# Moving x and g by 64 or 128 bytes in SBUF, with the weights left where they are

## The chip, the cores and the metric

The kernel runs on one core of a Trainium2 chip. The metric is the time of one execution in microseconds (us) on the device. Three runs of the kernel before gave 848.03, 845.73 and 847.87 us, a median of 847.87 us. TensorE (PE) does the matrix products, with its loads of the stationary operand shown apart as PEld; VectorE (DVE), ScalarE (ACT) and GpSimd (POOL) do the elementwise work; SyncE (SP) issues most transfers. SBUF is the on-chip memory that all of them read. An address in it here means the byte offset within a partition, which is the same in all 128 partitions.

## The reference

```
attn_out[b,h] = (scale * q k^T * D[h]) v          D[h][i,j] = gamma[h]**(i-j) for i >= j, else 0
x   = attn_out laid out as 2304 tokens x 512
h   = x @ w_in                                    2304 x 2048
g   = h * tanh(softplus(h))
y   = g @ w_out                                   2304 x 512
logits = y @ w_gate                               2304 x 8
every token goes to one of 8 experts, greedily by logit, at most 288 tokens to an expert
out[tokens of e] = relu(y[tokens of e] @ w1[e]) @ w2[e]
```

All of it is float32.

## The kernel before, in words

The program has two parts, one after the other. The first (`first_part`) computes the attention, the dense layer and the logits. The second (`second_part`) sorts the tokens to experts and runs the experts. No tile of the second part changes its address with this change.

Every float32 operand of the large products is split into a high part and a rest (names ending in h and l), both stored as fp32r, and a product is three products: high by high, low by high, high by low. One matmul is a load of a 128x128 stationary operand (LDWEIGHTS) and a stream of the moving operand through it (MATMUL).

The tokens are cut into 9 blocks of 256 (n = 0 to 8) and the hidden layer into 16 slices of 128 (f = 0 to 15). A pair (n, f) is a step; there are 144. `plan()` mixes the steps of blocks 0 to 2, since their weights are still arriving and being split; from block 3 on the blocks follow each other. A step issues:

- `ff_h` (line 317): 12 matmuls, 4 slices of the 512 inputs by 3 products. Stationary is a 128x128 piece of `winh[f]` or `winl[f]`, moving are 256 columns (1024 bytes) of `xh` or `xl`. They run in the order winh·xh, winl·xh, winh·xl.
- `ff_a1` to `ff_b3`: the activation g and its split into `gh` and `gl`, on ACT (lines 326 to 328 and 358), DVE (334, 339, 352) and POOL (346, 347, 359).
- `ff_y` (line 411), three steps later: 6 matmuls. Here a half of `gh` or `gl` is stationary and 512 columns (2048 bytes) of `woh[f]` or `wol[f]` move. In the last block `ff_y_last` (line 447) does it the other way round: 12 matmuls with pieces of the weights stationary and 256 columns of `gh` or `gl` moving.

The attention of a later block is put between the steps of an earlier one (lines 219 to 281). The order on each engine is the order in which the code is written.

The second part's expert products are line 1257 (stationary `wxh`/`wxl`, moving 288 columns, 1152 bytes, of `xth`/`xtl`) and line 1271 (the same with `hth`/`htl`).

The addresses come from pools that hand out tiles one behind the other. In the program before, all 64 weight tiles of the first part (`winh`, `winl`, `woh`, `wol`) begin at 160 modulo 256, and `xh`, `xl`, `gh`, `gl`, the temporaries `d` and `u`, `pm`, `y`, `att` and the raw weights at 96. A slice of x is 1024 bytes and a slice of a weight 512, so every piece read has the same remainder as its tile. In the second part a slice of `xth` or `hth` is 1152 bytes, four and a half times 256, so the slices begin in turn at 96 and at 224, and all stationary pieces begin at 96.

`x_block` gives each block its x: block 2 has its own two tiles in the pool `stage`, all others take turns on two buffers of the pool `work`.

Of the kernel before, what the change touches and what calls it, by code (L numbers as in the profile page):

```python
# [7 lines left out]
F32 = mybir.dt.float32  # L8
F32R = mybir.dt.float32r
# [9 lines left out]
P = 128  # L19
# [4 lines left out]
TB = 256  # L24
NB = N // TB
KT = DM // P
# [55 lines left out]
def first_part(ctx, tc, att, att_ht, att_hn, dtab, qtab, ktab, stab, wi, wo, wgb, ydram, L, constants, cst, begin, grid):  # L82
    nc = tc.nc
    big = ctx.enter_context(tc.tile_pool(name="big", bufs=1))
    work = ctx.enter_context(tc.tile_pool(name="work", bufs=1))
# [41 lines left out]
    for n, f in sorted([(i, f) for i, (n, f) in enumerate(steps) if n == 0 for f in (f, f + NF)],  # L127
                       key=lambda p: (p[0] + (WOL if p[1] >= NF else 0), p[1])):
        parts.append((wo[f - NF], woh[f - NF], wol[f - NF]) if f >= NF
                     else (wi[f], flat(winh[f]), flat(winl[f])))  # L130
    raws = []
    y0 = work.tile([P, 2, DM], F32, tag="y", name="y0")
    cvs = [y0[:, 0, :], y0[:, 1, :]]
    done = [0]
# [42 lines left out]
            nc.gpsimd.tensor_sub(self.lo, self.t, self.hi.bitcast(F32))  # L177

    xT = {}

    def x_block(n):
        if n not in xT:
            if n == 2:
                xT[n] = [sp.tile([P, KT, TB], F32R, tag="x2", name=f"x{k}2", bufs=2) for k in "hl"]
            else:
                xT[n] = [work.tile([P, KT, TB], F32R, tag="x" + k, name="x" + k, bufs=2) for k in "hl"]
        return xT[n]

    pm = {}
# [45 lines left out]
    def a_out(ci):  # L235
        b, s0, n = CHUNKS[ci]
        a = at_tiles[ci]
        qT = a[:, 0, 0:4 * n].rearrange("p (h t) -> p h t", h=4)
        p = pm[ci]
        xp = bank()  # L240
        for hp in range(4):
            if s0 > 0:
                nc.tensor.matmul(xp[:, hp, :n], SD[:, hp, :], qT[:, hp, :], start=(hp == 0), stop=False,
                                 skip_group_check=True)
        for hp in range(4):
            for s in range(2):
                h = 2 * hp + s
                nc.tensor.matmul(xp[s * 64:(s + 1) * 64, hp, :n], a[:n, 3, h * D:(h + 1) * D],  # L248
                                 p[:n, s, hp, :n], start=(s0 == 0 and hp == 0), stop=True,
                                 skip_group_check=True)  # L250
        tok = b * S + s0
        xh, xl = x_block(tok // TB)
        o = tok % TB
        nc.scalar.activation(xh[:, :, o:o + n], xp[:, :, :n], AF.Copy)
        nc.vector.tensor_sub(xl[:, :, o:o + n], xp[:, :, :n], xh[:, :, o:o + n].bitcast(F32))  # L255
# [53 lines left out]
    def ff_h(n, f, i):  # L309
        xh, xl = x_block(n)  # L310
        if i % 2 == 0:
            hbank[0] = psum.tile([P, 2, TB], F32, tag=("ph0", "ph1")[i // 2 % 2], name="ph")
        ph = hbank[0][:, i % 2, :]
        k = 0
        for kt in range(KT):
            for w, x in ((winh, xh), (winl, xh), (winh, xl)):
                nc.tensor.matmul(ph, w[f][:, kt, :], x[:, kt, :], start=(k == 0), stop=(k == 11))  # L317
                k += 1
        q2[n, f] = ph
# [211 lines left out]
    for i in range(len(steps) + YL):  # L531
# [13 lines left out]
        if new:  # L545
            n, f = steps[i]
# [873 lines left out]
def build(tc, ap, out):  # L1420
    nc = tc.nc
    with ExitStack() as ctx:
        pp = ctx.enter_context(tc.tile_pool(name="pp", bufs=1))
        dp = ctx.enter_context(tc.tile_pool(name="dp", bufs=1, space=bass.MemoryType.DRAM))
        cp = ctx.enter_context(tc.tile_pool(name="cp", bufs=1))
        ctx.enter_context(tc.manual_schedule())
        L = pp.tile([P, NT, E], F32, name="L")
        ydram = dp.tile([N, DM], F32, name="ydram")
        cst = {}
        start = []  # L1430
        cs = ExitStack()

        def begin():
            start.append(Search(cs, tc, L, cst))
            return start[0].early()

        with ExitStack() as c1:
            first_part(c1, tc, ap["att"], ap["att_ht"], ap["att_hn"], ap["dtab"], ap["qtab"],
                       ap["ktab"], ap["stab"], ap["wi"], ap["wo"], ap["wgb"], ydram, L, lambda: constants(cp, tc, ap, cst), cst, begin, lambda *a: Grid(cs, tc, L, cst).pieces(*a))
        keep = ctx.enter_context(tc.tile_pool(name="keep", bufs=1, reuse_waits="tile"))  # L1440
        L0 = keep.tile([P, NT, E], F32, name="L0")
        nc.gpsimd.tensor_copy(L0, L)
        with ExitStack() as c2:
            flag = second_part(c2, tc, L, ydram, ap["wx"], cst, out, start[0], True, L0)
            again = nc.values_load(flag[0:1, 0:1], min_val=0, max_val=1)
        cs.close()
        with tc.If(again != 0):
            with ExitStack() as c3:
                general_constants(c3, tc, ap, cst)
                second_part(c3, tc, L0, ydram, ap["wx"], cst, out, Start(c3, tc, L0, cst), False)  # L1450
# [91 lines left out]
```

## Time and profile before

| | us |
|---|---|
| median of three runs | 847.87 |
| the profiled execution | 849.51 |
| its span, first to last instruction | 847.6 |
| TensorE busy in the span | 776.6 |
| weight loads busy | 709.3 |
| DVE, ACT, POOL busy | 548.1, 437.3, 475.1 |

The profile shows one execution. Busy times overlap between engines. [...] A step of 12 matmuls on line 317 takes about 1.4 us from start to start of the next thing.

### The profile page before, as it was taken

The page shows a single profiled execution, that of the slowest core. Times are in us where ns is not written, and L with a number is a line of the kernel's source. Part 1 is how long each engine was busy: PE and PEld are TensorE (multiplying, and loading weights), DVE is VectorE, ACT ScalarE, POOL GpSimd, SP SyncE. Part 2 cuts the span into 40 slices and gives each one's busy share as a digit, 9 for nine tenths or more (in the row PEclk, how much of TensorE's full clock was granted, in tenths as well). Part 3 has the DMA queues.
Part 4 walks back from the last instruction along what each step waited for, and adds up shares of the span by engine and source line. Part 5 has one row for each costly group of instructions (what it writes and reads, how often), then busy time and mean ns, then how long its engine had stood idle before and what let it go on. Part 6 is the DMA issues. An engine that isn't in the chain of part 4 may idle for free.

```text
span 847.6 us, 16248 instructions
## 1 busy us (share of the span) xinstructions
PE 776.6 (92%) x6151; PEld 709.3 (84%) x6151; DVE 548.1 (65%) x1271; ACT 437.3 (52%) x963; POOL 475.1 (56%) x541
## 2 busy tenths in 40 slices
PE   6688878899999999999999999939999999999993
PEld 5677667788998888888888889929989899999993
DVE  4797989865545699797897885576566654442110
ACT  2677878754554545455455554423444543554520
POOL 2533333365544567676666665414777986977811
PEclk9799999999999999999999999958999999999997
DMA  8536343101204210120110000044555655655411
GB/s 313 174 111 201 137 135 125 50 27 51 75 26 150 76 50 26 61 82 34 51 50 26 1 26 2 2 147 163 171 181 178 194 168 174 177 159 175 128 30 32
DMA packets 27320, 87.63 MB, mean 103 GB/s; under 512 B 4448, under 2 KB 5600, under 8 KB 27104
## 3 DMA queue, kind: packets, MB, share of 16 engines
q1 hardware_dynamic: 24160, 77.06, 27.9%
q0 software_dynamic: 3072, 9.44, 3.5%
q8 instruction: 50, 0.82, 0.4%
q14 instruction: 38, 0.31, 0.1%
HBM read 77.05 MB, written 9.44 MB: 102 GB/s over the span
## 4 chain that ended last, share of the span: by engine, by line
PE 72%; DVE 9%; issue 6%; DMA 5%; ACT 4%; POOL 2%; SPq 0%; DVEq 0%; POOLq 0%; ACTq 0%
PE ph L317 20%; PE hp L1257 10%; PE op L1271 8%; PE b_E L411 8%; PE b_F L411 7%; DMA raw<-in_wi_dram 2%; PE cnt L972 2%; PE b_A L219 1%; DVE r L339 1%; PE b_D L248 1%; DVE raw L163 1%; DVE hot L868 1%; POOL wxl L811 1%; DMA raw<-in_wo_dram 1%; PE b_E L447 1%
## 5 line engine op out<-in xcount | busy, mean ns | idle before, releaser
L317 PE MATMUL ph<-xh,winh 128*128 128x256 f32 x576 | 164.9, 286 | 9.4 <-ACT d L326 6.7
L317 PE MATMUL ph<-xl,winh 128*128 128x256 f32 x576 | 162.9, 283 | 0.2 <-DVE xl L255 0.2
L317 PE MATMUL ph<-xh,winl 128*128 128x256 f32 x576 | 163.0, 283 | 0.0
L811 POOL TENSOR_TENSOR wxl<-wraw,wxh 128x1024 fp32r<-128x1024 f32 x60 | 142.4, 2396 | 30.5 <-ACT wxh L809 30.0
L359 POOL TENSOR_TENSOR gl<-u,gh 128x256 fp32r<-128x256 f32 x114 | 85.8, 753 | 88.3 <-ACT gh L358 87.6
L317 PEld LDWEIGHTS ph<-xh,winh 128*128 128x128 f32 x576 | 110.4, 192 | 20.2 <-ACT d L326 7.0
L326 ACT ACTIVATE d<-ph 128x256 f32<-128x256 f32 x144 | 54.8, 381 | 133.0 <-PE ph L317 117.3
L317 PEld LDWEIGHTS ph<-xh,winl 128*128 128x128 f32 x576 | 110.8, 192 | 4.5
L317 PEld LDWEIGHTS ph<-xl,winh 128*128 128x128 f32 x576 | 111.1, 193 | 0.4 <-DVE xl L255 0.4
L339 DVE RECIPROCAL u<-u 128x128 f32<-128x128 f32 x113 | 107.7, 953 | 3.9
L334 DVE TENSOR_TENSOR u<-d 128x128 f32<-128x128 f32 x113 | 45.4, 402 | 63.3 <-ACT d L328 55.5
L346 POOL TENSOR_TENSOR u<-d,u 128x128 f32<-128x128 f32 x112 | 52.3, 467 | 52.9 <-DVE u L339 52.8
L809 ACT ACTIVATE wxh<-wraw 128x1024 fp32r<-128x1024 f32 x64 | 67.3, 1052 | 18.5 <-DMA wraw<-in_wx_dram 18.5
L327 ACT ACTIVATE d<-d,half_b 128x256 f32<-128x256 f32 x144 | 73.5, 510 | 4.7
L347 POOL TENSOR_TENSOR u<-d,u 128x128 f32<-128x128 f32 x112 | 68.2, 609 | 8.8
L328 ACT ACTIVATE d<-d 128x256 f32<-128x256 f32 x144 | 60.2, 418 | 4.6
L358 ACT ACTIVATE gh<-u 128x256 fp32r<-128x256 f32 x144 | 57.9, 402 | 2.1 <-DVE u L352 2.0
L368 DVE SCALAR_TENSOR_TENSOR scr<-y,WG 128x512 bf16<-128x512 f32 x64 | 55.2, 863 | 0.4
L1248 DVE SCALAR_TENSOR_TENSOR htl<-hp,hth 128x288 fp32r<-128x288 f32 x64 | 28.4, 454 | 40.2 <-ACT hth L1260 37.9
L1260 ACT ACTIVATE hth<-hp 128x288 fp32r<-128x288 f32 x64 | 26.1, 408 | 51.9 <-PE hp L1257 46.7
L352 DVE SCALAR_TENSOR_TENSOR u<-u,ph 128x256 f32<-128x256 f32 x144 | 52.5, 365 | 0.3
L177 POOL TENSOR_TENSOR wol<-y,woh 128x512 fp32r<-128x512 f32 x16 | 20.6, 1288 | 53.5 <-ACT woh L174 53.5
(271 smaller groups left out, 1931.0 us busy)
## 6 DMA issues: line engine op xcount, KB each, us to landing
wraw<-in_wx_dram SPq DMA_DIRECT2D x64, 512.0 KB, 4.4
att<-in_att_dram SPq DMA_DIRECT2D x32, 512.0 KB, 5.4
raw<-in_wi_dram SPq DMA_DIRECT2D x16, 512.0 KB, 3.9
raw<-in_wo_dram SPq DMA_DIRECT2D x16, 512.0 KB, 3.2
ydram<-y SPq DMA_DIRECT2D x9, 512.0 KB, 2.8
WG<-in_wgb_dram SPq DMA_DIRECT2D x1, 2048.0 KB
att<-in_att_ht_dram SPq DMA_DIRECT2D x4, 256.0 KB, 4.4
att<-in_att_hn_dram SPq DMA_DIRECT2D x4, 256.0 KB, 4.8
```

The source lines that it names most:

```text
L317: nc.tensor.matmul(ph, w[f][:, kt, :], x[:, kt, :], start=(k == 0), stop=(k == 11))
L327: nc.scalar.activation(df, df, AF.Square, bias=half_b, scale=-0.5)
L328: nc.scalar.activation(df, df, AF.Copy, bias=0.5, scale=0.5)
L339: nc.vector.reciprocal(r, r)
L347: eng.tensor_mul(u[:, 0, :], d[:, 1, :], r)
L358: nc.scalar.activation(gh, g, AF.Copy)
L359: eng.tensor_sub(gl, g, gh.bitcast(F32))
L411: nc.tensor.matmul(py[n][t], g[:, t * P:(t + 1) * P], w[f], start=(f == 0 and w is woh and g is gh), stop=(f == NF - 1 and g is gl))
L809: nc.scalar.activation(hi, raw, AF.Copy)
L811: rest = lambda eng: eng.tensor_sub(lo, raw, hi.bitcast(F32))
L1257: nc.tensor.matmul(hp, W[kt][w][:, s], x[:, kt, :], start=(k == 0), stop=(k == 11))
L1271: nc.tensor.matmul(op, W[4 + ft // 2][w][:, s], h[:, ft, :], start=(k == 0), stop=(k == 23))
```

## The change

A tile of 64 bytes that nothing uses is put into the pool `work` ahead of `y0`. The two buffers of x are no longer handed out by the pool block by block; they are four tiles made once, and the second tile of the first pair has 128 bytes of padding behind it. What is written into them, who reads them and when is the same.

```
+    work.tile([P, 16], F32, name="between")
     y0 = work.tile([P, 2, DM], F32, tag="y", name="y0")
...
+    xs = [[work.tile([P, KT * TB + o], F32R, name=f"x{k}{j}")[:, :KT * TB].rearrange("p (k t) -> p k t", k=KT)
+           for k, o in (("h", 0), ("l", e))] for j, e in enumerate((32, 0))]
...
-                xT[n] = [work.tile([P, KT, TB], F32R, tag="x" + k, name="x" + k, bufs=2) for k in "hl"]
+                xT[n] = xs[n if n < 2 else (n + 1) % 2]
```

The addresses that follow, modulo 256, as the built programs have them:

| tiles | before | after |
|---|---|---|
| weights `winh`, `winl`, `woh`, `wol` | 160 | 160 |
| x of blocks 0, 3, 5, 7 | 96 | 160 |
| x of blocks 1, 4, 6, 8 | 96 | 32 |
| x of block 2, raw weights | 96 | 32 |
| `gh`, `gl`, `d`, `u`, `pm` | 96 | 32 |
| `y`, `y0` | 96 | 160 |
| `att`, all of the second part | 96 and others | the same |

So the moving operand of line 317 begins 64 bytes behind its stationary one modulo 256 before; after, it begins at the same remainder (blocks 0, 3, 5, 7) or 128 bytes away (the other blocks). For lines 411 and 447 the distance goes from 64 to 128 bytes.

Engine by engine the two programs hold the same instructions in the same order with the same shapes; x's tiles have other names. One wait differs: in the second part POOL waits for a mark of PE ahead of the product that writes `wxl7` and no longer ahead of the one before it, which writes `wxl6` (line 811).

## Rows read from the trace of the kernel before

**Rows 1.** The page: span, and busy time of TensorE.
```profile
span 847.6 us, 16248 instructions
...
PE 776.6 (92%) x6151; PEld 709.3 (84%) x6151; DVE 548.1 (65%) x1271; ACT 437.3 (52%) x963; POOL 475.1 (56%) x541
```
**Rows 2.** The page's chain of waits, shares by engine.
```profile
PE 72%; DVE 9%; issue 6%; DMA 5%; ACT 4%; POOL 2%; SPq 0%; DVEq 0%; POOLq 0%; ACTq 0%
```
**Rows 3.** Stretches of the span: busy us of each engine, clock, DMA.
```profile
core 0: us, PE busy (x) PEld busy (x) DVE busy (x) ACT busy (x) POOL busy (x), PEclk, DMA share, GB/s
0.00:200.00 200.00, 164.16 (x1175) 140.60 (x1176) 153.05 (x280) 133.71 (x306) 76.48 (x83) 0.95 0.39 135
200.00:500.00 300.00, 300.00 (x2289) 268.25 (x2288) 229.92 (x458) 154.16 (x382) 185.94 (x284) 1.00 0.16 54
500.00:545.00 45.00, 43.15 (x358) 42.01 (x357) 26.25 (x62) 23.85 (x59) 23.63 (x42) 1.00 0.04 13
```
**Rows 4.** What TensorE waited for from 200 to 545 us: total, times, longest.
```profile
PE b_D L638 <- DVE g_mm L634: 1.0, 1, 1.0
PE b_E L447 <- POOL gl L359: 0.5, 2, 0.3
PE b_E L447 <- ACT gh L358: 0.4, 1, 0.4
```
**Rows 5.** Groups on TensorE, 200 to 545 us: count, busy us, mean ns.
```profile
L317 PE MATMUL ph<-xh,winh 128*128 128x256 f32 x404 | 113.2, 280 | 0.0
L317 PE MATMUL ph<-xh,winl 128*128 128x256 f32 x404 | 112.8, 279 | 0.0
L317 PE MATMUL ph<-xl,winh 128*128 128x256 f32 x404 | 112.7, 279 | 0.0
```
**Rows 6.** Line 317 from 492.7 to 493.4 us: ns min/median/max, starts.
```profile
L317 PE MATMUL ph<-xl,winh x3: 277/277/277, 492.4 to 493.1; 128*128 128x256 f32 x3
L317 PE MATMUL ph<-xh,winh x3: 276/276/277, 492.6 to 493.2; 128*128 128x256 f32 x3
```
**Rows 7.** Line 317 from 515 to 540 us, the same columns.
```profile
L317 PE MATMUL ph<-xh,winh x36: 280/281/282, 516.1 to 539.7; 128*128 128x256 f32 x36
...
L317 PE MATMUL ph<-xh,winl x36: 281/282/282, 516.2 to 539.9; 128*128 128x256 f32 x36
```
**Rows 8.** Timeline of TensorE around 493 us: start us, us.
```profile
492.32 0.28 PE L317 MATMUL ph<-xh,winl 128*128 128x256 f32 x1
...
493.57 0.39 PE L411 MATMUL b_E<-woh,gh 128*128 128x512 f32 x1
...
494.95 0.28 PE L317 MATMUL ph<-xh,winh 128*128 128x256 f32 x1
```
**Rows 9.** Timeline of TensorE around 517 us.
```profile
516.07 0.28 PE L317 MATMUL ph<-xh,winh 128*128 128x256 f32 x1
...
517.49 0.28 PE L447 MATMUL b_E<-gh,woh 128*128 128x256 f32 x1
```
**Rows 10.** Line 411 from 200 to 500 us: ns min/median/max, starts.
```profile
L411 PE MATMUL b_F<-wol,gh x86: 387/394/398, 199.8 to 499.8; 128*128 128x512 f32 x86
L411 PE MATMUL b_E<-woh,gl x85: 388/392/452, 200.0 to 497.2; 128*128 128x512 f32 x85
```
**Rows 11.** Line 447 from 500 to 545 us, the same columns.
```profile
L447 PE MATMUL b_E<-gh,wol x29: 276/281/283, 502.4 to 544.3; 128*128 128x256 f32 x29
```
**Rows 12.** Timeline of TensorE in the second part, around 820 us.
```profile
815.11 0.68 PE L1257 MATMUL hp<-xtl,wxh 128*128 128x288 f32 x4
...
819.27 1.20 PE L1271 MATMUL op<-hth,wxh 128*128 128x288 f32 x8
...
823.43 0.30 PE L1271 MATMUL op<-hth,wxl 128*128 128x288 f32 x1
```
**Rows 13.** Line 1271 from 819.6 to 823.3 us: ns min/median/max.
```profile
L1271 PE MATMUL op<-hth,wxl x8: 291/292/293, 820.3 to 821.2; 128*128 128x288 f32 x8
```
**Rows 14.** Line 811 from 540 to 600 us: ns min/median/max.
```profile
L811 POOL TENSOR_TENSOR wxl<-wraw,wxh x4: 2384/2394/2402, 582.2 to 590.8; 128x1024 fp32r<-128x1024 f32 x4
```

## The prediction

> **What bounds the kernel now.** I read the stretches of the span first. [...] Before 200 us TensorE is busy for 164 of 200 us [rows 3], and the chain there runs through transfers, DVE and ACT as well as matmuls, so I count nothing for it. The second part begins when the first has ended, and none of its tiles moves, so what the first part gains or loses should arrive at the end in full. Over the span the chain is 72% TensorE [rows 2], which is busy 776.6 us [rows 1].
>
> Then I read how long matmuls of one shape take, since the change can only act there. Line 317 has 3 x 404 = 1212 matmuls from 200 to 545 us, of 279.3 ns on average [rows 5]. They come in two levels. Around 493 us they take 276 or 277 ns [rows 6], and 11 of them start within 493.57 - 492.32 = 1.25 us [rows 8], one per 113.6 ns. From 516 us on they take 280 to 282 ns [rows 7], and 12 start within 517.49 - 516.07 = 1.42 us [rows 9], one per 118.3 ns. The addresses are the same at both levels, modulo 256, so the level isn't set by the address alone. Going by the durations, (279.3 - 276.5) / (281.5 - 276.5) = 0.56 of the 1212 are at the slow level, and the mean distance is 113.6 + 0.56 x 4.7 = 116.2 ns.
>
> **What the change touches.** No instruction is added, removed or moved. The change can act in four ways.
>
> *Line 317.* The moving x begins 64 bytes from its stationary weights modulo 256 before, and 0 (blocks 3, 5, 7) or 128 bytes away after (blocks 4, 6, 8). No row of the first part shows such a distance, but the second part does: its moving slices begin at 96 and 224 in turn, and all its stationary pieces at 96. There 64 matmuls of 288 columns start from 815.11 to 823.43 us [rows 12], one per 130.0 ns, half at distance 0 and half at 128, and the durations lie within 291 to 293 ns [rows 13], so the two distances cannot be far apart. To bring 130.0 ns to 256 columns I take the cost of a column from lines 411 and 317 of one stretch: six matmuls of 512 columns start within 494.95 - 493.57 = 1.38 us, 230.0 ns each [rows 8]; (230.0 - 113.6) / 256 = 0.455 ns a column, 14.6 ns for 32 columns. At the slow level it is (230.0 - 118.3) / 256 = 0.436 ns, 14.0 ns. So line 317 would take 115.4 to 116.0 ns a matmul after; I take 115.7, against 116.2 now: 1212 x -0.5 = -0.6 us. The bounds are the two levels seen at this shape: all fast, 1212 x (113.6 - 116.2) = -3.2 us; all slow, 1212 x (118.3 - 116.2) = +2.5 us. It is nearest to the middle because the two halves of the blocks get the two distances in equal number.
>
> *Lines 411 and 447.* Line 411 has about 6 x 85.5 = 513 matmuls from 200 to 500 us, with a median near 394 ns, a least of 387 and a most of 398 in a typical group [rows 10]. Its distance goes from 64 to 128. Bounds: 513 x -7 ns = -3.6 us, 513 x +4 ns = +2.1 us. No row shows this shape at another distance, and the spread lies on both sides, so I take 0. Line 447 (172 matmuls, median 281, least 276, most 283 [rows 11]) can gain 172 x 5 ns = 0.9 us or lose 172 x 2 ns = 0.3 us; I take 0.
>
> *DVE, ACT, POOL and the transfers.* Their tiles move by 64 or 128 bytes too. From 200 to 545 us TensorE waits 1.9 us for them, and a gain or loss there hides behind it. Elsewhere DVE, ACT and POOL hold 9 + 4 + 2 = 15% of the chain [rows 2], 127 us. No row shows one operation at two such addresses; the nearest is the spread of equal POOL products, 2384 to 2402 ns, 0.8% [rows 14], which bounds it at ±1.0 us. I take 0, as the shapes and the number of bytes stay.
>
> *The wait that POOL shifts.* It is for a mark of PE from the first part and stands before products that start at 582 us or later [rows 14], long after line 317 has ended. It costs nothing in either place; behind it on POOL stand only the later products of line 811 and the expert gathers.
>
> **The sum.** -0.6 us. The profiled execution took 849.51 us, 847.6 of span and 1.9 around it, and would become 848.9. It lies 1.6 us above the median of the runs, 847.87; off that median the forecast is 847.3 us. The outer bounds added are -3.2 - 3.6 - 0.9 - 1.0 = -8.7 us and +2.5 + 2.1 + 0.3 + 1.0 = +5.9 us.
>
> The trace shows that a load of weights runs beside nearly every matmul, PEld 268 of 300 us [rows 3], and that equal matmuls at equal addresses differ by 4.7 ns. [...]
>
> [...]
>
> **The rivals.**
>
> *Faster: the fast level holds.* If the slow level comes from the moving stream meeting the weight load at a fixed distance of 64 bytes, the new distances could avoid it. Then line 317 and line 447 run at the fast level (-3.2 and -0.9 us), and line 411 gains up to its best (-3.6 us): 847.9 - 4.1 = 843.8 us, or 840.2 us with all of line 411. For it: the levels hold for long stretches without a change in the work, from 516 to 540 us for one [rows 7], as a fixed pattern of two reads would. Against it: the second part runs at 0 and 128 and is not at a rate that would be the fast level (130.0 - 14.6 = 115.4 against 113.6). It decides from 0.8 of the 1212 at the fast level on with some gain on line 411; line 317 alone at the fast level is just 3.2 us.
>
> *Slower: distance 128 pins the slow level.* Half the blocks' line 317, and all of lines 411 and 447, get distance 128. If that is the bad one, these products run at the slow level or above: 606 x +2.1 = +1.3 us on blocks 4, 6 and 8, +2.1 us on line 411, +0.3 us on line 447, and should distance 0 be bad as well another +1.3 us: 851.6 to 852.9 us. For it: the second part's 115.4 to 116.0 ns is a mean over both distances, and one half could hide a worse one. Against it: durations there spread by 2 ns only [rows 13]. It decides once line 411 joins; line 317 alone stays within the noise.
>
> *The address changes what others do.* If the reads of TensorE meet those of DVE, ACT and POOL, all of which moved along, the levels would fall elsewhere but in the same mixture: within 1 us of 847.9, the forecast's side.
>
> **How the numbers follow.** What a measurement of this kernel can tell from no change is about 0.3%, 2.5 us; the runs shown span 2.3 us. No change that can be told, with the rule of the ports and the last rival in it: 0.44, at 847.3 us, its own range 845.3 to 850.3 us. Faster, 0.33: the levels are seen, and 840 to 845 us is within reach of them. Slower, 0.23: its bounds are nearer. The range of 842.0 to 851.5 us leaves out a deeper gain (about 0.1) and the slower rival at its worst (about 0.08).
>
> **What would show it.** Right: line 317 from 200 to 545 us at a mean of 278.5 to 279.5 ns, blocks at distance 0 and at 128 within 3 ns of each other, line 411 near 394 ns, and TensorE still without a gap. Wrong towards faster: a mean of 277 ns or less, or a median of line 411 at 390 ns or below. Wrong towards slower: 281 ns or more, line 411 at 397 ns or more. If matmuls stay as they are and the time moves by over 2.5 us, the cause is not on TensorE in that stretch and the whole reading is wrong.

## The result: 851.2 us, and the profile after

The kernel after took 851.2 us in the median (849.37 to 853.57, eight runs), against 847.87 us before (eight runs); the ratio of the means is 1.0051, with a 95% interval of 1.0037 to 1.0065. The kernel after is slower by 3.3 us between the medians and by 4.3 us, 0.5%, between the means, where no change was forecast.

TensorE has no gap after either. The stretches of the kernel after, with the columns of [rows 3]:

```profile
200.00:500.00 300.00, 300.00 (x2266) 268.64 (x2265) 227.40 (x454) 152.28 (x376) 184.02 (x280) 1.00 0.16 54
500.00:545.00 45.00, 43.63 (x360) 42.80 (x358) 25.73 (x60) 24.05 (x60) 23.66 (x43) 1.00 0.04 13
```

It is as busy as before and does less: 2266 matmuls from 200 to 500 us, where it was 2289 [rows 3]. The clock is the same 1.00, so the matmuls themselves follow each other more slowly. Their durations on line 320, which was line 317, from 200 to 545 us (ns min/median/max, first and last start):

```profile
L320 PE MATMUL ph<-xh,winh x402: 276/283/285, 199.8 to 542.4; 128*128 128x256 f32 x134
L320 PE MATMUL ph<-xh,winl x402: 279/283/287, 199.9 to 542.5; 128*128 128x256 f32 x134
L320 PE MATMUL ph<-xl,winh x402: 274/283/290, 200.0 to 542.6; 128*128 128x256 f32 x134
```

The median of all three is 283 ns, above the most that the slow level showed before [rows 7]. The starts say by how much: matmuls of 283 ns that start some 120 ns apart overlap, so the pace is the time from start to start. Four starts in the kernel after: a step of block 6 (x at distance 128) from its first matmul to what follows it, and one of block 7 (distance 0):

```profile
430.20 0.28 PE L320 MATMUL ph<-xh,winh 128*128 128x256 f32 x1
...
431.64 0.40 PE L414 MATMUL b_E<-woh,gh 128*128 128x512 f32 x1
...
451.25 0.28 PE L320 MATMUL ph<-xh,winh 128*128 128x256 f32 x1
...
452.68 0.49 PE L246 MATMUL b_D<-att,sd 128*128 128x128 f32 x3
```

12 matmuls in 1.44 us and in 1.43 us: 120.0 and 119.2 ns each, against 113.6 and 118.3 at the two levels of before [rows 8, 9]. Line 414, which was 411, hardly moves; from 200 to 500 us it has, beside [rows 10],

```profile
L414 PE MATMUL b_F<-wol,gh x84: 390/392/393, 208.1 to 499.2; 128*128 128x512 f32 x84
L414 PE MATMUL b_E<-woh,gl x84: 390/396/398, 208.3 to 499.4; 128*128 128x512 f32 x84
```

with medians of 392 and 396 where they were 394 and 392.

One number serves to compare all kernels below: the time from the first matmul of block 3 to the first matmul of the last step, 95 steps later. TensorE runs through it with next to no wait: from 200 to 545 us it waited 1.9 us before [rows 4] and 1.4 us after. The timeline of the kernel before at these two places:

```profile
220.55 0.28 PE L317 MATMUL ph<-xh,winh 128*128 128x256 f32 x1
...
538.68 0.28 PE L317 MATMUL ph<-xh,winh 128*128 128x256 f32 x1
```

and of the kernel after:

```profile
219.37 0.28 PE L320 MATMUL ph<-xh,winh 128*128 128x256 f32 x1
...
541.33 0.28 PE L320 MATMUL ph<-xh,winh 128*128 128x256 f32 x1
```

318.1 us became 322.0 us, +3.8 us. From the starts in the trace, line 317's matmuls in blocks 3 to 8 go from a mean of 116.2 to 119.2 ns, line 411's from 230.6 to 231.3 (where nothing stands between them) and line 447's from 116.6 to 118.9. In the stretch that is 1140 x 3.0 = 3.4 us, 498 x 0.7 = 0.3 us and 144 x 2.3 = 0.3 us: some 4 us for 3.8. The two profiled spans differ by 1.7 us only, since block 3 began 1.2 us earlier after, and from the last step to the end of the span it took 0.9 us less; in the medians of the runs 3.3 us stand.

The starts also show a rhythm for each distance between the addresses. In blocks 3, 5 and 7, at distance 0, 87% of the matmuls follow the one before by 119 to 121 ns. In blocks 4, 6 and 8, at 128, the times from start to start go 117, 120, 123, 117, 120, 123, or 115, 117, 122, 120, 119. Both have a mean of 119.2 ns. Before, they were mostly 113 to 114 or 117 to 118 for many matmuls on end.

### The profile page after: what moved, and what is told of

The parts are those of the page before. It is cut to its first block, busy times and chain, and to the rows that moved or that the text cites. A ratio compares the mean times of both kernels' runs of the same rounds, so it can differ in the third digit from the quotient of the medians.

```text
span 849.3 us, 16248 instructions
## 1 busy us (share of the span) xinstructions
PE 782.8 (92%) x6151; PEld 714.6 (84%) x6151; DVE 547.6 (64%) x1271; ACT 438.0 (52%) x963; POOL 475.4 (56%) x541
## 4 chain that ended last, share of the span: by engine, by line
PE 71%; DVE 10%; issue 6%; DMA 5%; ACT 4%; POOL 2%; SPq 0%; DVEq 0%; POOLq 0%; ACTq 0%
PE ph L320 20%; PE hp L1260 9%; PE op L1274 8%; PE b_E L414 8%; PE b_F L414 7%; DMA raw<-in_wi_dram 2%; PE cnt L975 2%; DVE r L342 2%; PE b_A L222 1%; PE b_D L251 1%; DVE raw L164 1%; DVE hot L871 1%; DMA raw<-in_wo_dram 1%; PE b_E L450 1%; PE b_F L450 1%
## 5 line engine op out<-in xcount | busy, mean ns | idle before, releaser
L329 ACT ACTIVATE d<-ph 128x256 f32<-128x256 f32 x144 | 55.0, 382 | 137.2 <-PE ph L320 117.0
L1260 PE MATMUL hp<-xth,wxh 128*128 128x288 f32 x256 | 50.1, 308 | 0.9 <-DVE htl L1251 0.9
```

The source lines that it names most:

```text
L1260: nc.tensor.matmul(hp, W[kt][w][:, s], x[:, kt, :], start=(k == 0), stop=(k == 11))
```

## The experiments

Theory: the time of a 256-column matmul goes by the distance, modulo 256, between the address of the moving operand and that of the stationary pieces being loaded. Rivals: x's own address modulo 256; the form of x's tiles, made once; the moved tiles of the other engines. All edits are made to the kernel before, if nothing else is said. Each ratio is one of means, against the kernel before run beside it, whose medians were 848.95 us (e1 to e4), 846.89 (e5 to e8), 848.36 (e9 to e12) and 848.85 us (e13, e14). "Stretch" is the time just defined, and each run's two starts stand behind it. A remainder written as a distance is moving minus stationary on line 317; "behind" is negative.

**e1_static: the new tiles without the new addresses.**

```
-    work.tile([P, 16], F32, name="between")          (from the kernel after)
-    ... enumerate((32, 0))]
+    ... enumerate((0, 0))]
```

> The kernel after with both paddings taken out: x in four tiles made once, every address as before (x and g at 96). If the addresses do it: line 317 (here L319) at 116.2 ns a matmul from 200 to 545 us as before, and 847.9 us, ratio 1.000. If the form of x's tiles did it: 119.2 ns a matmul as in the kernel after, and 851 us, ratio 1.005.

849.05 us against 848.95, ratio 1.0002 (0.9990 to 1.0015); line 317 at 116.2 ns. Stretch 318.2 us:

```profile
220.61 0.28 PE L319 MATMUL ph<-xh,winh 128*128 128x256 f32 x1
...
538.80 0.28 PE L319 MATMUL ph<-xh,winh 128*128 128x256 f32 x1
```

The form of the tiles costs nothing.

**e2_dist0 and e3_dist128: one distance for all blocks.**

```
+    work.tile([P, 16], F32, name="between")          e3: 48
     y0 = work.tile([P, 2, DM], F32, tag="y", name="y0")
```

> The kernel before with 64 bytes of padding ahead of y0 alone: x and g at 160, distance 0 to the weights in all blocks and in lines 411 and 447. If the distance modulo 256 between moving and stationary sets it: line 317 in every block as blocks 3, 5 and 7 of the kernel after, an even 120 ns with a mean of 119.2, so 1212 x 3.0 ns = +3.6 us, ratio about 1.004. If only distance 128 is bad: 116 ns or less and 848 us or below. If it is the moving of the other engines' tiles: between 848 and 851 us with line 317 at 116 ns.

> The kernel before with 192 bytes of padding ahead of y0 alone: x and g at 32, distance 128 everywhere. If the distance sets it: line 317 in every block as blocks 4, 6 and 8 of the kernel after, 117, 120 and 123 ns in turn with a mean of 119.3, +3.7 us, ratio about 1.004. If only distance 0 is bad: 116 ns and 848 us.

Distance 0: 853.69 us, ratio 1.0062 (1.0047 to 1.0077), line 317 at 119.3 ns. The second and third line below are the first matmuls of two steps of its last block, one step apart (12 matmuls of line 317 and 12 of line 447); the first and last line bound its stretch of 322.1 us:

```profile
219.99 0.28 PE L318 MATMUL ph<-xh,winh 128*128 128x256 f32 x1
...
519.01 0.28 PE L318 MATMUL ph<-xh,winh 128*128 128x256 f32 x1
...
521.89 0.28 PE L318 MATMUL ph<-xh,winh 128*128 128x256 f32 x1
...
542.05 0.28 PE L318 MATMUL ph<-xh,winh 128*128 128x256 f32 x1
```

24 matmuls in 2.88 us are 120.0 ns each, in a place where the kernel before ran at 118.3 [rows 9]. Distance 128: 854.5 us, ratio 1.0067 (1.0052 to 1.0081), 119.3 ns, stretch 322.4 us:

```profile
221.81 0.28 PE L318 MATMUL ph<-xh,winh 128*128 128x256 f32 x1
...
544.23 0.28 PE L318 MATMUL ph<-xh,winh 128*128 128x256 f32 x1
```

Both distances are bad, and equally so.

**e4_shift_all: new addresses, old distance.**

```
+    big.tile([P, 16], F32, name="ahead")
     winh = [big.tile([P, KT, P], F32R, name=f"winh{i}") for i in range(NF)]
```

> The kernel before with 64 bytes of padding ahead of the first weight: weights at 224, x, g and all behind at 160, so that x lies where it lies in blocks 3, 5 and 7 of the kernel after, but at the old distance of 64 to the weights. If the distance sets it: 116.2 ns a matmul and 847.9 us, ratio 1.000. If x's own address modulo 256 sets it (160 is bad, 96 good): 119.2 ns and 851.5 us, ratio 1.004.

849.1 us, ratio 1.0005 (0.9993 to 1.0018), line 317 at 116.3 ns, stretch 318.3 us:

```profile
220.22 0.28 PE L318 MATMUL ph<-xh,winh 128*128 128x256 f32 x1
...
538.54 0.28 PE L318 MATMUL ph<-xh,winh 128*128 128x256 f32 x1
```

With x at 160, where the kernel after has it in half its blocks, nothing is lost so long as the weights stand 64 bytes further on. The distance counts, not x's own address.

**e5 to e9: the other distances.** The edit is that of e2_dist0 with 32, 8, 24 and 40 in place of 16; for 96 behind, `half_b` is made ahead of `winh` and nothing else is changed.

> The kernel before with 128 bytes of padding ahead of y0: x and g at 224, that is 64 bytes ahead of the weights modulo 256, where they were 64 behind. If what counts repeats every 128 bytes (0 and 128 alike, as measured at 119.2 and 119.3 ns): line 317 as before, 113.5 and 118 ns in turn with a mean of 116, ratio 1.000. If 64 behind is one good place in 256: 119 ns or more, ratio 1.004 or more.

> The kernel before with 32 bytes of padding ahead of y0: x and g at 128, 32 behind the weights modulo 256. If the cost falls evenly from distance 0 to distance 64: between 116.2 and 119.2 ns a matmul, 117.7, ratio 1.002. If the cost comes in steps of 64 bytes: 116.2 or 119.2 ns, ratio 1.000 or 1.004.

> The kernel before with 96 bytes of padding ahead of y0: x and g at 192, 32 ahead of the weights. If the sign of the distance plays no part: as with 32 behind. If it does, this differs from 32 behind by more than 1 ns a matmul on line 317.

> The kernel before with the 4-byte tile half_b made ahead of the weights instead of behind them: weights at 192, x and g at 96 still, 96 behind modulo 256. If the cost repeats every 128 bytes, 96 behind is 32 ahead: the same mean on line 317 as in the run at 32 ahead, within 0.5 ns. If it repeats every 256 only, no such match.

> The kernel before with 160 bytes of padding ahead of y0: x and g at 0, 96 ahead of the weights modulo 256, the last of the eight distances in steps of 32. If every distance has its own mean, as the seven measured so far: between 116.1 and 119.4 ns a matmul on line 317, ratio 1.000 to 1.007, and 64 behind stays the best. If 96 ahead lies between its neighbours 64 ahead (117.8) and 128 (119.3): 118.5 ns, ratio 1.005.

The starts, in the order e5, e6, e7, e8, e9, and then all eight distances (g moves with x; lines 411 and 447 as above):

```profile
220.44 0.28 PE L318 MATMUL ph<-xh,winh 128*128 128x256 f32 x1
...
541.39 0.28 PE L318 MATMUL ph<-xh,winh 128*128 128x256 f32 x1
```
```profile
221.53 0.28 PE L318 MATMUL ph<-xh,winh 128*128 128x256 f32 x1
...
542.45 0.28 PE L318 MATMUL ph<-xh,winh 128*128 128x256 f32 x1
```
```profile
221.01 0.28 PE L318 MATMUL ph<-xh,winh 128*128 128x256 f32 x1
...
540.63 0.28 PE L318 MATMUL ph<-xh,winh 128*128 128x256 f32 x1
```
```profile
220.98 0.28 PE L318 MATMUL ph<-xh,winh 128*128 128x256 f32 x1
...
542.75 0.28 PE L318 MATMUL ph<-xh,winh 128*128 128x256 f32 x1
```
```profile
221.37 0.28 PE L318 MATMUL ph<-xh,winh 128*128 128x256 f32 x1
...
544.73 0.28 PE L318 MATMUL ph<-xh,winh 128*128 128x256 f32 x1
```

| distance | kernel | line 317, ns | line 411 | line 447 | stretch, us | ratio (95%) |
|---|---|---|---|---|---|---|
| -96 | e8 | 118.5 | 233.2 | 118.4 | 321.8 | 1.0062 (1.0043 to 1.0081) |
| -64 | before | 116.2 | 230.6 | 116.6 | 318.1 | 1 |
| -32 | e6 | 118.4 | 231.6 | 118.0 | 320.9 | 1.0053 (1.0039 to 1.0068) |
| 0 | e2 | 119.3 | 231.4 | 119.6 | 322.1 | 1.0062 (1.0047 to 1.0077) |
| 32 | e7 | 117.0 | 232.8 | 116.8 | 319.6 | 1.0023 (1.0010 to 1.0036) |
| 64 | e5 | 117.8 | 233.5 | 117.8 | 321.0 | 1.0057 (1.0043 to 1.0071) |
| 96 | e9 | 120.2 | 232.9 | 119.8 | 323.4 | 1.0075 (1.0059 to 1.0091) |
| 128 | e3 | 119.3 | 231.8 | 118.6 | 322.4 | 1.0067 (1.0052 to 1.0081) |

64 behind, where the kernel before stands, is the best of the eight, and the only one with a stretch at 113 to 114 ns; 64 ahead has 117 to 118 throughout. So what counts repeats neither every 64 nor every 128 bytes: 96 behind and 32 ahead differ by 1.5 ns. The expectation that the cost falls evenly from 0 to 64 behind was wrong: 32 behind, at 118.4, is close to distance 0. Of the other forecasts, that 32 ahead and 32 behind differ by more than 1 ns came true (e7); e5 fits neither of its two, and e9, at 120.2, lies above the most that was expected of it. The ratios are up to 0.2% above what the stretches give (e3: 4.3 of 848 us is 0.5%, measured 0.67%). For e5 to e8 some of that lies in the kernel before, which ran 1.5 to 2.1 us faster beside them than beside the others. For the rest no cause is shown: in e3's trace block 3 begins 1.3 us later than before (221.81 against 220.55 us), but in the trace of the kernel after, whose line 317 is as slow in blocks 0 to 2 (119.0 ns), 1.2 us earlier.

**e10_g_only: the other tiles alone.** Behind x's tiles 192 bytes are left free, so that g, d and u lie as in the kernel after, with x in place (but for block 2).

```
     a_out(0)
+    work.tile([P, 48], F32, name="between")
```

> The kernel before with 192 bytes of padding behind x: x of all blocks but 2 stays at 96, g, d and u move to 32 as in the kernel after. If line 317's reads of x carry the loss: 116.2 ns a matmul on line 317, 231.2 on line 411, 119 on the last block's line 447 (192 x 2.3 ns = 0.4 us), ratio 1.000 to 1.001. If the moving of g, d and u carries it: ratio 1.003 or more.

849.39 us, ratio 1.0008 (0.9998 to 1.0018), stretch 318.7 us:

```profile
220.75 0.28 PE L317 MATMUL ph<-xh,winh 128*128 128x256 f32 x1
...
539.49 0.28 PE L317 MATMUL ph<-xh,winh 128*128 128x256 f32 x1
```

Line 447 went to 118.9 ns, as in the kernel after, line 411 stayed at 230.3. Line 317 took 119.3 ns in block 2, whose x had moved to distance 128, and 117.1 and 116.2 ns in blocks 3, 5, 7 and 4, 6, 8, whose x had not. The loss is line 317's reads of x. (`y` and `pm`, which move in the kernel after, stay in place here.)

**e11_xl_p32 and e12_xl_0: a part of the stream at another distance.** The low part of x gets a pool of its own, behind `work`, with a pad ahead.

```
+    apart = ctx.enter_context(tc.tile_pool(name="apart", bufs=1))
+    apart.tile([P, 24], F32, name="between")         e12: 16
...
-    ... work.tile(...) for k in "hl"]
+    ... p.tile(...) for p, k in ((work, "h"), (apart, "l"))]
```

> The kernel before with the low part of x in a pool of its own at 192, 32 ahead of the weights; the high part of x stays at 96, 64 behind, and g at 96. Only the third of line 317's matmuls that moves xl changes its distance. If each matmul's time goes by its own distance: 116.2 ns for two thirds and 117.0 for xl's, a mean of 116.5, ratio 1.000. If the stream of matmuls falls into one rhythm that all distances make together: another mean, for xh's matmuls as well, between 113.6 (which would be -3 us, ratio 0.996) and 119 ns.

> The same with the low part of x at 160, distance 0, the high part at 96. If each matmul's time goes by its own distance: 116.2 ns where xh moves, 119.2 where xl moves, a mean of 117.2, ratio 1.001. If the stream falls into one rhythm: xh's matmuls leave 116.2 too, anywhere from 113.6 to 120 ns.

e11: 851.03 us, ratio 1.0032 (1.0019 to 1.0044), line 317 at 118.5 ns, stretch 321.2 us. e12: 851.11 us, ratio 1.0039 (1.0025 to 1.0052), 118.2 ns, stretch 320.5 us. The starts of e11, then of e12:

```profile
219.92 0.28 PE L319 MATMUL ph<-xh,winh 128*128 128x256 f32 x1
...
541.09 0.28 PE L319 MATMUL ph<-xh,winh 128*128 128x256 f32 x1
```
```profile
219.34 0.28 PE L319 MATMUL ph<-xh,winh 128*128 128x256 f32 x1
...
539.82 0.28 PE L319 MATMUL ph<-xh,winh 128*128 128x256 f32 x1
```

In e11 no distance in the stream is worse than 117.0 when it stands alone, and the mixture is at 118.5, the matmuls that move xh among it: their medians are 118 and 119 ns, 117 before. So a matmul's time isn't its own distance's price, and the theory, which holds for a stream of one distance, doesn't add up over a mixed one. In e11 the largest rise is right ahead of the matmuls that move xl, where the stream changes from xh to xl: 119.8 ns, 116.0 before; in e12 it is about as large ahead of them (119.1) as behind them (118.7, 115.8 before). Whether each change of distance costs something, or the whole stream falls into another rhythm, these two runs don't tell.

**e13_fine_56_48 and e14_fine_72_80: finer than 32 bytes.** x is one tile in a pool of its own, cut some bytes from its start.

```
+    flatx = apart.tile([P, 4 * KT * TB + 8], F32R, name="x")
...
+    xs = [[flatx[:, (2 * j + i) * KT * TB + o:(2 * j + i + 1) * KT * TB + o].rearrange("p (k t) -> p k t", k=KT)
+           for i in range(2)] for j, o in enumerate((2, 4))]      e14: (6, 4), and half_b ahead of winh
```

> The kernel before with x in one tile of a pool of its own, cut 8 bytes from its start for blocks 0, 3, 5, 7 (x at 104, 56 behind the weights) and 16 bytes for blocks 1, 4, 6, 8 (x at 112, 48 behind); g at 96 as before. If the cost goes by the exact distance and falls evenly from 32 to 64 behind (118.4 to 116.1 ns): 116.7 ns in blocks 3, 5, 7 and 117.3 in blocks 4, 6, 8, ratio 1.001. If only the 32-byte step counts: 116.1 in both, ratio 1.000. If 64 behind is not the best place: one half below 115.5 ns, ratio 0.999 or less.

> The same with the 4-byte tile half_b made ahead of the weights, so that the weights are at 192; x is cut 24 bytes from its start for blocks 0, 3, 5, 7 (x at 120, 72 behind) and 16 for blocks 1, 4, 6, 8 (x at 112, 80 behind). g stays at 96, now 96 from the weights. If the cost rises evenly from 64 to 96 behind (116.1 to 118.5): 116.7 and 117.3 ns. If only the 32-byte step counts: 118.5 in both. If a finer optimum is on this side: one half below 115.5. Line 411 at about 233 ns and line 447 at 118.4, as at 96 behind, which costs some 1.3 us whatever line 317 does.

e13: 853.28 us, ratio 1.0059 (1.0046 to 1.0072), stretch 321.8 us; 120.0 ns at 56 behind and 119.2 at 48. e14: 854.64 us, ratio 1.0069 (1.0055 to 1.0084), stretch 322.8 us; 119.7 ns at 72 and 119.1 at 80 behind (two gaps of 214 ns left out). In e14 the first buffer's `xl` ends 8 bytes behind the start of the second's `xh`, so that two columns are overwritten and the results are wrong; of it only the starts of matmuls are read. The starts of e13, then of e14:

```profile
220.01 0.28 PE L321 MATMUL ph<-x,winh 128*128 128x256 f32 x1
...
541.83 0.28 PE L321 MATMUL ph<-x,winh 128*128 128x256 f32 x1
```
```profile
220.98 0.28 PE L322 MATMUL ph<-x,winh 128*128 128x256 f32 x1
...
543.76 0.28 PE L322 MATMUL ph<-x,winh 128*128 128x256 f32 x1
```

All four are worse than 64, 32 and 96 behind, so neither the even rise nor the 32-byte step holds, and none of these four places is a finer optimum.

In e11 to e14 a part of x or all of it lies in another pool, and no run has it there at 64 behind, so that the place alone could be a rival. Block 2 speaks against it: its x lies in a third pool, which moves along, and line 317 took there 117.3 ns in e11 (32 ahead), 118.9 in e12 (distance 0), 118.3 in e13 (32 behind) and 115.6 in e14 (x at 128, 64 behind weights at 192), each within 0.6 ns of the table; the last is the good distance a third time at other addresses. No arrangement tried beats the kernel before.

## Why the prediction was wrong

- *What bounds the kernel.* The sums take a nanosecond on a matmul's start for a nanosecond on the span, and that was right. From 200 to 500 us TensorE is busy for 300.00 of 300 us before and after, from 200 to 545 us it waits 1.9 us before [rows 3, 4] and 1.4 us after, and where the stretch lost 3.8 us, the median of the runs rose by 3.3 us.
- *Line 317* is the step that failed. It was put at 115.7 ns after, -0.6 us, with a ceiling of all matmuls at the slow level, +2.5 us. It took 119.2 ns, which by the prediction's own count is 1212 x 3.0 = +3.6 us, above that ceiling. Two things were wrong in it. The second part's 130.0 ns [rows 12] was taken over by a cost per column; by such a cost, (231.3 - 119.2) / 256 = 0.438 ns, the 119.2 ns measured here would be 133.2 ns at 288 columns, so the two streams don't convert into each other. The second part's stream changes between distances 0 and 128 at every matmul, and e11 and e12 show that a mixed stream doesn't take the mean of its distances (118.5 and 118.2 ns, where by the table the means are 116.5 and 117.2); that this is the reason here is argued, not shown. And the slow level was taken as the most that this shape can cost, where it was the most at one distance: e2, e3 and e9 run at 119.3 to 120.2 ns.
- *Equal addresses at two levels, so the level is not set by the address alone* was true and led astray. It is the distance that decides which levels there are (113.5 and 118 at 64 behind, 120 at 0, 118 alone at 64 ahead), and which of them is taken at 64 behind stays open.
- *Lines 411 and 447* were put at 0, with -4.5 to +2.4 us as bounds. By the starts they cost 513 x 0.7 and 172 x 2.3 ns, 0.4 us each.
- *DVE, ACT, POOL, the transfers, and POOL's wait* at 0: e10 bounds `g`, `d`, `u` and the raw weights, together with line 447 and block 2's x, at 1.0008 (0.9998 to 1.0018).
- *The chance of 0.44* takes in a "rule of the ports", with no change in the time. No run shows such a rule. The runs show loads of weights busy beside the matmuls, 268.64 of 300 us after, and line 317 going from 116.2 to 119.2 ns by a change of addresses alone (with the new tiles at the old addresses, e1, it stays at 116.2).
- *The slower rival* was the nearest, with 128 bad and "should distance 0 be bad as well". Its terms were not right: with both distances bad its sum is 852.9 us, of which line 411 makes +2.1 us, where it cost 0.4, and line 317 +2.6 us, where it cost 3.6. *The faster rival* failed: the new distances did away with the fast level, and no step of line 317 in the kernel after is faster than 118.2 ns a matmul.
- *The range.* That 851.2 us lies within 842.0 to 851.5 is luck: the slower rival reached its 851.6 us, with 128 alone bad, by line 411 at +2.1 us and not by line 317.
- *The signs to look for* counted on durations. For the kernel after, line 317's pointed the right way (a mean of 282 ns, over the 281 that was to mean slower). But they are a poor measure: at 64 ahead (e5) the mean duration of line 317 is 279 ns as before [rows 5], while the starts are 1.6 ns further apart.

The cause is shown: the distance between the addresses of x and the weights, in steps below 256 bytes (e2 and e3 at 119.3 ns against e4 at 116.3), acting on line 317 (e10: 119.3 ns in the block whose x moved, 117.1 and 116.2 in those whose x did not). That it repeats every 256 bytes is not shown: by the addresses of the built programs, all pairs compared here at one distance also have the same distance modulo 512. What in the chip makes the distance count, no run shows, nor what moves the stream from one level to the other at 64 behind.

## What to carry to other kernels

In this kernel, where TensorE is the bound (300.00 of 300 us busy) and matmuls of 256 columns stream with a new load of weights each, the distance between the moving and the stationary address, in steps below 256 bytes, is worth some 3% of their time (116.2 to 120.2 ns) and up to 0.75% of the kernel's (e9). In a kernel like it a pad of 32 to 192 bytes is a cheap thing to try in steps of 32, and a pad added for another reason is worth a second measurement: 64 bytes cost 0.62% here (e2). Which distance is good there is not known from here. Read the pace from the starts of matmuls, not from their durations: at 64 ahead (e5) the mean duration is the 279 ns of before, and the starts are 1.6 ns further apart. A level seen at one address was no bound for another: the slow level at 64 behind was 118.3 ns [rows 9], and 0, 128 and 96 ahead run at 119.3 to 120.2.

## What the hardware showed that was not expected

- Eight distances in steps of 32 bytes have paces from 116.2 to 120.2 ns for 256 columns, without an order that the distance would suggest. 0 and 128 agree (119.3 ns), and so do 96 and 32 behind (118.5 and 118.4).
- The paces are rhythms: mostly 120 at distance 0; 117, 120, 123 in turn at 128; 116, 118, 120, 113 in most steps at 32 ahead (e7); 118, 121, 116, 125, 116, 124 in turn at 96 ahead (e9), where one matmul of some 133 stands in 46 of the 96 steps.
- x off the 32-byte grid cost more than any neighbour on it: 119.1 to 120.0 ns at 48, 56, 72 and 80 behind, against 118.5, 116.2 and 118.4 at 96, 64 and 32 behind.
